# Soft-capped attention and a leaky MLP on one core: grouped score steps, another layout for batch 1's q and k, and weight bounds from squares

## The chip, the cores and the metric

The kernel runs on one core of a Trainium2 chip. The metric is the device time of one execution in microseconds (us); the time of before is the median of three runs.

## The reference

```python
scores = scale * np.matmul(q, k.transpose(0, 1, 3, 2))   # 4 batches x 12 heads, 448 x 448, head_dim 64
scores = cap * np.tanh(scores / cap)
attn = np.exp(scores - scores.max(-1, keepdims=True))
attn = attn / (attn.sum(-1, keepdims=True) + 1e-09)
x = np.matmul(attn, v)            # then (4, 448, 768) -> 1792 tokens of 768
h = x @ w_in                      # 768 x 2048
g = np.maximum(h, 0.0) + alpha * np.minimum(h, 0.0)
out = (g @ w_out).astype(np.float32)
```

All inputs but the weights and alpha are float32; w_in and w_out arrive as float64 and are turned into float32 in the kernel with shifts on VectorE (`to_f32`, lines 973 to 997).

## The kernel before, in words

**Precision.** The large products (`mm1` with w_in, line 878, and `mm2` with w_out, line 920) multiply numbers that are split into a high and a low 16-bit part, three products for each. Weights, x and the hidden values are first scaled by powers of two. So each operand needs a bound of its size: of q and k for batches 2 and 3, of v for each batch (`vbatch`, line 485), and of each 128-wide chunk of the weights (`norms`, line 999).

**Bounds of the weights.** For a chunk of 128 x 768, six bf16 products of the chunk with itself on TensorE (`gram`, line 1003) leave a 128 x 128 matrix in PSUM; ScalarE then sums its absolute values row by row (`bound`, line 387, with an accumulator). There are 32 chunks, 16 of w_in and 16 of w_out, in eight groups of four. The bound of v is the largest absolute value of each load, by a VectorE reduction (line 499), six for each batch.

**From 128 partitions to one number.** `allmax` (line 395) turns a column of maxima with a transpose on TensorE (line 408), reduces on VectorE (line 404), and sends the result to all partitions with a float32 product with `ones` (line 411). It is called 22 times.

**Attention.** Two heads make a unit (a "pair", six for each batch). A score step computes 128 rows of both heads of a unit (`step`, line 560): products on TensorE into one of two PSUM buffers, tanh on ScalarE (line 579), a maximum on VectorE (line 583), exp on ScalarE (line 590). The 64 rows left over in a unit of 448 rows are put together with those of the next unit in one step with four quadrants ("tail"). There are 42 steps in batches 0 and 1, in float32 (`scores_32`, line 547), and 42 in batches 2 and 3, in split form (`scores_3`, line 553). Each step is one operation of the plan on TensorE. For batches 0 and 1 q and k are loaded as (head, position, d) and turned by float32 products of 64 columns with the identity (`turn`, line 510), two heads at a time in the two column halves of the array: eight such products for 448 rows of q or k. The attention weights are turned either on TensorE (`turn_32`, line 658, batch 0 and the first two units of batch 1) or, from there on, split on ScalarE, VectorE and GpSimd and turned by DMA (`turn_split`, line 635).

**Splitting.** A split in "direct" form is a scaled high part (any of three engines) and one VectorE operation for the low part (line 437). In the other form it is a scaling in place, a copy, and a subtraction that VectorE or GpSimd may take (lines 646 to 648 and 691 to 693). The shares `PA`, `QA` and `VA` (lines 68, 69 and 77) say what part of the blocks of the attention weights, of q and k, and of v takes the direct form.

**The order.** The program is written out ahead by a list scheduler (`Plan`, line 92). Each operation has a priority (`prio` plus an offset `OFF[tag]`, line 82), estimated durations for each engine that may do it, and regions that it reads and writes. At each moment every engine takes the ready operation of the lowest number. SP issues all loads and stores in the order that the plan gives. Where TensorE has nothing to do in the first part, the plan puts in products that nobody reads (`fill`, line 1146).

**Stages.** Batch 0's attention (with w_in, w_out and batch 1's attention beside it), then `mm1` of batch 0, and so on, with the next batch's attention beside the products of the last.

Of the kernel before, what the change touches and what calls it, by code (L numbers as in the profile page):

```python
# [10 lines left out]
F32 = mybir.dt.float32  # L11
# [14 lines left out]
VM = 0  # L26
NM = 1.0
MQ = 3
AQ = 3
PEN = 9557.32  # L30
PEN2 = -1671.74
PENP = 5200.84
B0_P = 93.34
LD_P = -164.74
LO_P = 1000.92
MM_P = 4281.34
X_P = 315.24
ST_P = 16.4
ST1_P = -45.43
PV_P = 472.96  # L40
QK_P = -151.82
V_P = 260.72
WI_P = 61.01
WI_S = -61.06
A_S = 2.7
MM1_P = 318.9
WO_P = -214.34
WO_S = 99.12
WT_P = -410.5
WT_S = 70.95  # L50
B1_P = 663.99
B_S = 274.91
EVAC_P = -855.04
# [28 lines left out]
OFF = [-65.0, 6.9, 224.8, 851.3, 36.2, -180.9, 44.9, -286.1, -175.0, -265.3, 4.4, 117.7, -15.8, 9.2, -390.3, 0.0, 45.0, -62.9, -109.4, 120.6, -265.2, -349.8, 24.6, -515.1, -49.0, 243.8, -1013.8, -3.5, 43.4, 0.0, -77.0, 123.3, 26.1, 120.4, 29.4, -6.2, 15.4, -212.7, -27.4, 0.0, 60.8, 7.6, 0.0, 254.3, 178.4, 5.0, -87.7, 524.0, 70.1, 161.5, 27.5, -55.8, -195.2, -115.0, 0.0, 126.1, 302.1, -51.9, -333.5, -18.9, 0.5, 53.5, -114.5, -86.3, -14.4, -100.4, 284.8, 177.1, -107.8, 3.9, -157.6, -54.5, 125.4, -8.7, 0.0, 14.8, 0.0, -119.3, 23.0, -192.0, -212.7, -149.3, -12.4, 18.2, 71.8, 186.2, 0.0, -86.2, 0.0, -5.0, 77.7, 438.7, 44.3, 0.0, 0.6, -1145.9, 37.7, -11.3, -250.4, -182.1, -181.5, 256.2, -26.1, -60.8, -11.1, 107.6, -898.5, 92.5, -382.7, -110.3, -4.1, 24.0, 40.1, -4.5, -27.2, 39.1, -77.6, -13.4, 4.7, 0.0, 67.6, 91.6, 107.9, -4.9, 19.1, -11.5, -4.6, 0.0, 19.9, 16.4, 211.6, -17.2, -23.8, 8.2, -0.7, 74.9, 21.2, -96.8, 0.0, -124.2, -8.4, 3.6, -807.4, 16.1, 0.0, -25.4, 0.0, 108.1, -97.6, -0.3, -72.3, 1276.7, 808.9, -325.6, 158.2, -634.9]  # L82
# [9 lines left out]
class Plan:  # L92
# [16 lines left out]
    def op(self, prio, times, fn, r=(), w=(), rows=1.0, port=True, mode=0):  # L109
        o = lambda: None  # L110
        o.prio, o.times, o.fn, o.rows, o.idx, o.port, o.mode = prio + OFF[self.tag], times, fn, rows, len(self.ops), port, mode
# [24 lines left out]
    def order(self):  # L136
# [55 lines left out]
        while todo:  # L192
# [10 lines left out]
            for e in free:  # L203
# [3 lines left out]
                while ready[e]:  # L207
# [4 lines left out]
                    if not fits(o) or e == "dve" and o.port and port["pool"] > now:  # L212
                        skipped.append(item)
                        continue
                    for h in o.handles:
                        if h.slot is None:
                            h.slot = banks.pop(0)
                            used[h.kind] += 1
                            if h.kind == "m":
                                self.line.pop(0)  # L220
# [7 lines left out]
                    elif e == "pe":  # L228
                        free[e] = run_pe(t + (SWITCH if o.mode and o.mode != mode else 0.0), o.rows)
# [37 lines left out]
def kernel(  # L267
# [79 lines left out]
    ones = ct([NF, P], F32, "ones")  # L347
# [9 lines left out]
    junk = ct([P, 512], mybir.dt.uint8, "junk")  # L357
# [29 lines left out]
    def bound(e, o, i, func=AF.Abs):  # L387
        if e == "act":
            nc.scalar.activation(out=junk[:i.shape[0], :i.shape[1]], in_=i, func=func, accum_out=o)
        else:  # L390
            absmax(o, i)

    mxt_no = [0]

    def allmax(prio, src, rows, r, first, w):
# [7 lines left out]
        def reduce(e):  # L403
# [7 lines left out]
        op(prio, {"pe": 310}, lambda e: nc.tensor.matmul(  # L411
            ps_p[h.slot][:, 256:256 + m], ones[:m], diag if m > 1 else top, start=True, stop=True), r=[tr], w=[h])
# [40 lines left out]
    def load(prio, dst, src, b, pair, w):  # L453
        op(prio, {"sp": (550, 1400, 1000)}, lambda e: nc.sync.dma_start(out=dst.rearrange("p (h c) -> p h c", h=2),  # L454
# [8 lines left out]
    def loads32():  # L463
        for pair in range(NPAIR):
            n = 2 * NCH * D
            for i, src in ((4, k), (6, q)):
                o = pair % 3 * n
                t = wpair[i + pair // 3].rearrange("p a b -> p (a b)")[:CP, o:o + n]
                raw32[i, pair] = t, (("wp", i + pair // 3), o, o + n)
                load(QK_P + A_S * pair, t, src, 0, pair, [raw32[i, pair][1]])  # L470
# [13 lines left out]

    def vbatch(b):
# [8 lines left out]
        op(prio, {"dve": 30}, lambda e: nc.vector.memset(t[:, :NPAIR], 0.0), w=[(u.tok, 0, 9)])  # L494
        for pair in range(NPAIR):
            rv, m = vslot(b, pair)
            v0[b, pair] = rv, m
            load(prio + 0.4 * pair, rv, v, b, pair, [m])
            op(prio + 0.4 * pair, {"act": 830} if b < VM else {"dve": 680}, lambda e, pair=pair, rv=rv: bound(e, t[:CP, pair:pair + 1], rv, AF.Square),
               r=[m], w=[(u.tok, pair, pair + 1)] + [("junk", 0, 1)] * (b < VM), port=False)  # L500
# [37 lines left out]
    def t0_slot(i):  # L538

        if i % 5 < 4:  # L540
# [3 lines left out]
                    [(("g", r // 2), r % 2 * GW + lo, r % 2 * GW + lo + 2 * CP) for r in range(a, a + 8)])  # L544
        return pt32[:, -2 * S:].rearrange("p (c j k) -> p c j k", c=2, j=NCH), [("pt", 10 * S, 12 * S)]
# [13 lines left out]

    def step(u, pr, col, routes, scale):  # L560
# [4 lines left out]
        units = [r[0] for r in routes[0]]  # L565

        def products(e):
            for fns in zip(*(u.scores(s, x, *r) for x in range(2) for r in routes[x])):
                for fn in fns:
                    fn()  # L570

# [625 lines left out]
```

## Time and profile before

| | |
|---|---|
| median of 3 runs | 683.25 us (683.14 to 683.63) |
| the profiled execution, its own time | 686.12 us |
| its span | 684.3 us |
| granted clock, mean | 0.995 |
| instructions | 13548 |

How to read the rows further down: "busy" is the time in which at least one instruction of the engine was under way; for TensorE ("PE") matmuls overlap, so the cost of a group of matmuls is better read from the time between its start and the start of the next group in the timeline. A float32 product appears as two records. DVE is VectorE, ACT is ScalarE, POOL is GpSimd, SPq is the queue of SyncE, which issues the DMAs.

### The profile page before, as it was taken

The numbers are of one execution on the slowest core, as the hardware profiler recorded it, in microseconds if no ns is written. First come the engines' busy times: TensorE is split into PE (matmuls) and PEld (weight loads), VectorE is DVE, ScalarE is ACT, GpSimd is POOL, SyncE is SP. The second block draws the span as 40 slices with busy tenths as digits, with TensorE's granted clock in tenths as the row PEclk, the third lists the DMA queues.
The fourth block names the chain that finished last, engine by engine and source line by source line (L and its number), as shares of the span: only waits on it lengthen the run. The fifth ranks groups of instructions, "written<-read, shape, count | busy, mean of one in ns | idle before, by whom it ended". The sixth has DMA issues, their size and how long they took to land.

```text
span 684.3 us, 13548 instructions
## 1 busy us (share of the span) xinstructions
PE 666.8 (97%) x5151; PEld 413.4 (60%) x5151; DVE 481.7 (70%) x922; ACT 395.4 (58%) x853; POOL 237.4 (35%) x354
## 2 busy tenths in 40 slices
PE   8998998989999999999999999999999999999997
PEld 7787776768877555544555555545455555555664
DVE  3998999999989977687898577878877504441000
ACT  5887797885857666476575546756756513331100
POOL 1145755335656532264433234444432200000000
PEclk9999999999999999999999999999999999999999
DMA  8995674366664369937749989766466640000011
GB/s 176 292 323 154 203 235 115 102 194 178 159 125 85 39 140 205 185 62 137 139 77 179 197 167 181 139 139 122 91 136 116 106 73 22 1 0 1 24 46 24
DMA packets 181792, 87.07 MB, mean 127 GB/s; under 512 B 145312, under 2 KB 178016, under 8 KB 181728
## 3 DMA queue, kind: packets, MB, share of 16 engines
q1 hardware_dynamic: 181728, 86.22, 56.9%
q8 instruction: 40, 0.66, 0.4%
q14 instruction: 24, 0.20, 0.1%
HBM read 45.82 MB, written 5.51 MB: 75 GB/s over the span
## 4 chain that ended last, share of the span: by engine, by line
PE 66%; DVE 19%; DMA 6%; ACT 3%; SPq 3%; issue 2%; POOL 1%; ACTq 0%; DVEq 0%; POOLq 0%
PE p L886 27%; PE p L927 24%; PE p L711 4%; DVE mxs L583 4%; PE s L557 3%; DMA ptall<-pw 3%; PE p L738 2%; DVE wp L437 2%; PE s L551 2%; SPq L454 1%; DVE wi L437 1%; DVE wp L992 1%; DVE wp L986 1%; PE p L515 1%; SPq L847 1%
## 5 line engine op out<-in xcount | busy, mean ns | idle before, releaser
L886 PE MATMUL p<-xring,wi 128*128 128x448 f16 (+2 forms) x1440 | 225.8, 315 | 0.3 <-DVE gr L896 0.3
L927 PE MATMUL p<-wp,gall 128*128 128x384 f16 x1344 | 224.9, 326 | 0.4 <-DVE gr L896 0.4
L886 PEld LDWEIGHTS <-wi 128*128 128x128 f16 x1440 | 134.7, 98 | 84.2 <-issue 5.7
L927 PEld LDWEIGHTS <-gall 128*128 128x128 f16 x1344 | 129.2, 98 | 90.7 <-issue 7.3
L590 ACT ACTIVATE tall<-tall,mxs 128x448 f32<-128x448 f32 x126 | 82.7, 659 | 15.1 <-POOL mxs L585 9.8
L896 DVE SCALAR_TENSOR_TENSOR gr<-p,ca_g,gr 128x448 f32<-128x448 f32 (+2 forms) x80 | 46.9, 586 | 47.7 <-ACT gr L427 47.4
L585 POOL TENSOR_SCALAR mxs<-mxs,small 128x2 f32<-128x2 f32 x62 | 33.3, 537 | 99.1 <-DVE mxs L583 69.3
L583 DVE TENSOR_REDUCE mxs<-tall 128x2 f32<-128x896 f32 x63 | 66.9, 1075 | 1.0 <-ACT tall L579 0.9
L427 ACT ACTIVATE gr<-p,cs_g 128x448 f32<-128x448 f32 (+2 forms) x63 | 34.7, 551 | 56.0 <-PE p L886 53.3
L434 POOL TENSOR_TENSOR gall<-gr,gall 128x192 f16<-128x192 f32 (+4 forms) x52 | 45.0, 869 | 33.0 <-ACT gall L421 21.7
L437 DVE SCALAR_TENSOR_TENSOR pw<-tall,rr,pw 128x448 f16<-128x448 f32 x56 | 41.1, 735 | 14.1 <-ACT pw L427 12.4
L579 ACT ACTIVATE tall<-s,ams 128x896 f32<-128x896 f32 x42 | 41.1, 1000 | 14.6 <-PE s L557 6.0
L434 POOL TENSOR_TENSOR pw<-tall,pw 128x448 f16<-128x448 f32 x33 | 38.7, 1173 | 26.6 <-ACT pw L421 25.1
L427 ACT ACTIVATE wp<-p,small 128x384 f32<-128x384 f32 x19 | 10.9, 576 | 55.3 <-PE p L927 55.3
L421 ACT ACTIVATE gall<-gr 128x384 f16<-128x384 f32 (+4 forms) x51 | 24.2, 477 | 30.7 <-DVE gr L896 30.6
L711 PE MATMUL p<-ptall,vs 112*64 112x448 f16 x384 | 40.3, 355 | 0.2 <-issue 0.2
L607 POOL TENSOR_SCALAR rr<-sums 128x2 f32<-128x2 f32 (+2 forms) x70 | 27.6, 394 | 29.5 <-ACT tall L590 22.3
L427 ACT ACTIVATE pw<-tall,rr 128x448 f16<-128x448 f32 x27 | 17.9, 665 | 27.2 <-DMA ptall<-pw 23.2
L711 PEld LDWEIGHTS <-vs 112*64 112x64 f16 x384 | 21.2, 110 | 17.3 <-issue 3.7
L434 DVE TENSOR_TENSOR gall<-gr,gall 128x384 f16<-128x384 f32 (+4 forms) x60 | 28.4, 478 | 4.1 <-ACT gall L421 1.6
L421 ACT ACTIVATE ptall<-p 112x512 f32<-112x512 f32 (+1 forms) x48 | 26.3, 580 | 6.5 <-PE p L665 5.3
L421 ACT ACTIVATE pw<-tall 128x448 f16<-128x448 f32 x37 | 21.2, 574 | 14.5 <-DMA ptall<-pw 12.6
(155 smaller groups left out, 961.5 us busy)
## 6 DMA issues: line engine op xcount, KB each, us to landing
wp<-in_moe_w_in_dram SPq DMA_DIRECT2D x16, 768.0 KB, 7.6
wp<-in_moe_w_out_dram SPq DMA_DIRECT2D x16, 768.0 KB, 5.2
rvs<-in_v_dram SPq DMA_DIRECT2D x38, 224.0 KB, 3.4
rqk<-in_q_dram SPq DMA_DIRECT2D x18, 224.0 KB, 3.2
rqk<-in_k_dram SPq DMA_DIRECT2D x18, 224.0 KB, 3.4
ptall<-pw SPq DMA_TRANSPOSE x128, 3.2
wp<-in_k_dram SPq DMA_DIRECT2D x6, 224.0 KB, 5.7
wp<-in_q_dram SPq DMA_DIRECT2D x6, 224.0 KB, 6.0
```

The lines of the kernel that those rows point to most:

```text
L421: nc.scalar.activation(out=o, in_=i, func=AF.Copy)
L427: nc.scalar.activation(out=o, in_=i, func=AF.Copy, scale=s)
L434: (nc.gpsimd if e == "pool" else nc.vector).tensor_tensor(out=o, in0=a, in1=b, op=ALU.subtract)
L437: nc.vector.scalar_tensor_tensor(out=o, in0=i, scalar=s, in1=hi, op0=ALU.mult, op1=ALU.subtract)
L579: op(pr, {"act": (152 if reg else 245) + 377 * 2}, lambda e: nc.scalar.activation(out=t, in_=s[:, :, :S].rearrange("p c (j k) -> p c j k", ...
L583: op(pr, {"dve": 136 + 469 * 2}, lambda e: nc.vector.tensor_reduce(out=mt, in_=t, axis=AX.XY, op=ALU.max), r=tr, w=[mr], port=False)
L585: op(pr, {"dve": 200, "pool": 265}, lambda e: (nc.gpsimd if e == "pool" else nc.vector).tensor_scalar(out=mt, in0=mt, scalar1=ncap, scalar ...
L590: nc.scalar.activation(out=t[:, x], in_=t[:, x], func=AF.Exp, scale=capr, bias=mt[:, x:x + 1], accum_out=sums[:, u.idx % 3, col + x:col + ...
L711: nc.tensor.matmul(pv[x * D:(x + 1) * D, :n], vs[:, z, c:c + D], u.pt[x][:CP, y * NCH + kc], start=(i == 0), stop=(i == len(prods) - 1))
L886: nc.tensor.matmul(ps_p[h.slot][:, :n], w[:, z, kk, :], x[:, d, o:o + n], start=(kk == 0 and z == d), stop=(kk == NPAIR - 1 and z == 1))
L896: op(pr, {"dve": 198 + 1.07 * n}, lambda e: nc.vector.scalar_tensor_tensor(out=t, in0=ps_p[h.slot][:, :n], scalar=ca_g[:, j:j + 1], in1=t, ...
L927: nc.tensor.matmul(ps_p[h.slot][:, :NH], g[j][:, d, t * P:(t + 1) * P], w[:, z, hf * NH:(hf + 1) * NH], start=(j == 0 and z == d), stop=(j ...
```

## The change

- One operation of the plan computes the products of up to two score steps in a row (`products`, with `PAIR = (1, 1)`); tails stay single and come after the group that holds the second unit's first step. The turns of the attention weights are put into the plan unit by unit.
- The plan, when TensorE would change the shape of its tiles, takes a ready operation of the present shape whose priority is at most `SAME` behind.
- Batch 1's q and k are loaded with the two heads side by side, with one DMA per head, and turned by four transposes.
- The weight bounds: 24 of 32 chunks (half of w_in, all of w_out) are squared and summed on ScalarE; the other eight keep their products, and a VectorE maximum reads them.
- The bound of v for batches 0 and 1 (`VM = 2`) comes from products of v with itself on TensorE and one VectorE maximum for several loads.
- `ones` and the second operand of its product are bf16.
- `QA` 1 to 0, `VA` 1 to 0.5, `PA` 0.5 to 0.25: fewer splits in direct form.
- Each load of q, k, v and of the weights has a priority offset of its own; all constants and offsets of the plan have new values.
- The stores of the fourth token tile are one DMA instead of two; `cap` is loaded from ScalarE's queue.

```diff
-VM = 0
+VM = 2
-QA = 1.0
-VA = 1.0
+QA = 0
+VA = 0.5
+SAME = 209.56
+LOAD_C = (600, 1400, 950)
+SPLIT_W = (0.5, 1)
+PAIR = (1, 1)
-PA = 0.5
+PA = 0.25
...
+                    if e == "pe" and mode and o.mode != mode:
+                        top = item[0] + SAME
+                        while ready[e] and ready[e][0][0] <= top:
+                            x = heapq.heappop(ready[e])
+                            if x[2].mode == mode and fits(x[2]):
+                                skipped.append(item)
+                                item, o = x, x[2]
+                                break
+                            skipped.append(x)
...
-    ones = ct([NF, P], F32, "ones")
+    ones = ct([NF, P], BF16, "ones")
...
-        op(prio, {"pe": 310}, lambda e: nc.tensor.matmul(
-            ps_p[h.slot][:, 256:256 + m], ones[:m], diag if m > 1 else top, start=True, stop=True), r=[tr], w=[h])
+        op(prio, {"pe": 100}, lambda e: nc.tensor.matmul(
+            ps_p[h.slot][:, 256:256 + m], ones[:m], (diag if m > 1 else top).bitcast(BF16).rearrange("p (m t) -> p m t", t=2)[:, :, 1],
+            start=True, stop=True), r=[tr], w=[h])
...
+    def gram_v(prio, o, w, tops):
+
+        h = plan.handle("n")
+
+        def gram(e):
+            for i, (top, _) in enumerate(tops):
+                for c in range(NCH):
+                    nc.tensor.matmul(ps_p[h.slot][:, :P], top[:, c, :, 1], top[:, c, :, 1],
+                                     start=(i == c == 0), stop=(i == len(tops) - 1 and c == NCH - 1))
+
+        op(prio, {"pe": 230 * len(tops)}, gram, r=[m for _, m in tops], w=[h], rows=0.875)
+        op(prio, {"dve": 280}, lambda e: absmax(o, ps_p[h.slot][:, :P]), r=[h], w=[w], port=False)
...
+            if b < VM:
+                tops.append((rv.bitcast(BF16).rearrange("p (c f t) -> p c f t", f=P, t=2), m))
+                if len(tops) == (2 if b else NPAIR):
+                    gram_v(prio + 0.4 * pair, t[:, pair:pair + 1], (u.tok, pair, pair + 1), tops)
+                    tops = []
+                continue
...
+    def products(pr, steps):
+
+        sr = [(("S", (step_no[0] + z) % 2), 0, 1) for z in range(len(steps))]
+
+        def run(e, i0=step_no[0]):
+            for z, (u, _, _, routes, _) in enumerate(steps):
+                s = ps_s[(i0 + z) % 2]
+                for fns in zip(*(u.scores(s, x, *r) for x in range(2) for r in routes[x])):
+                    for fn in fns:
+                        fn()
...
+        groups = []
+        while line:
+            k_ = 2 if PAIR[us[0].b > 0] else 1
+            groups.append(line[:k_])
+            line = line[k_:]
+        if m:
+            a, tail = us[0], slice(n - m, n)
+            at = next(i for i, g_ in enumerate(groups) if g_[-1][0] is us[1] or (i + 1 < len(groups) and groups[i + 1][0][0] is us[1]))
+            groups.insert(at + 1, [(a, a.prio + st_p * nf, nf, [[(v, y, slice(x * QP, (x + 1) * QP), tail) for x, v in enumerate(us)] for y in range(2)], a.joint)])
...
+        for dst, src, w in ((rq, q, rqr), (rk, k, rkr)):
+            if scores32:
+                for h in range(2):
+                    op(prio - 20, {"sp": LOAD_C}, lambda e, h=h, dst=dst, src=src: nc.sync.dma_start(
+                        out=dst.rearrange("p (c h d) -> p h c d", h=2, d=D)[:, h],
+                        in_=src[b, 2 * pair + h].rearrange("(p c) d -> p c d", c=NCH)), w=[(w[0], w[1] + h / 2, w[1] + (h + 1) / 2)])
+            else:
+                load(prio - 20, dst, src, b, pair, [w])
...
-                op(prio - i, {"pe": 205 * NCH}, lambda e, h=h, raw=raw: turn(h, raw, 0, NCH), r=[rr_, identr], w=[h, w], rows=0.7, mode=1)
+                def turn_c(e, h=h, raw=raw):
+                    for c in range(NCH):
+                        nc.tensor.transpose(ps_p[h.slot][:, c * CP:(c + 1) * CP], raw[:, c * P:(c + 1) * P], ident[:CP, :CP])
+
+                op(prio - i, {"pe": TURN * NCH}, turn_c, r=[rr_, identr], w=[h, w])
...
+        grams = []
+        for i, (flat, fr) in enumerate(flats):
+            sq = share(norm_no[0] % NF, SPLIT_W[norm_no[0] // NF])
+            norm_no[0] += 1
+            if sq:
+                op(prio, {"act": 195 + 0.833 * DM}, lambda e, i=i, flat=flat: nc.scalar.activation(
+                    out=junk, in_=flat, func=AF.Square, accum_out=n[:, i:i + 1]), r=[fr], w=[(nr[0], nr[1] + i, nr[1] + i + 1), ("junk", 0, 1)], port=False)
+            else:
+                grams.append((i, flat, fr))
+        if not grams:
+            return
...
+        op(prio, {"dve": 150 + 130 * m}, lambda e: absmax(n[:, i0:i0 + st * (m - 1) + 1:st], ps_p[h.slot][:, :m * P].rearrange("p (m f) -> p m f", f=P)),
+           r=[h], w=[(nr[0], nr[1] + i, nr[1] + i + 1) for i, _, _ in grams], port=False)
...
+        if t == 3:
+            p0, both_b = 3 * P - (NCH - 1) * CP, out[(b - 1) * S:(b + 1) * S].rearrange("(i p c) e -> c i p e", i=2, c=NCH)
+            op(EVAC_P, {"sp": (550, 1000, 800)}, lambda e: nc.sync.dma_start(
+                out=both_b[NCH - 1, :, p0:, a], in_=osb[:, a]), r=[osr])
+            return
...
-    nc.sync.dma_start(out=capt, in_=cap.to_broadcast([P, 1]))
+    nc.scalar.dma_start(out=capt, in_=cap.to_broadcast([P, 1]))
```

## Rows read from the trace of the kernel before

**Rows 1.** Chain that ended last, by engine, from the page.
```profile
PE 66%; DVE 19%; DMA 6%; ACT 3%; SPq 3%; issue 2%; POOL 1%; ACTq 0%; DVEq 0%; POOLq 0%
```
**Rows 2.** Busy time by stretches: stretch and length, engines, clock, DMA.
```profile
20.00:240.00 220.00, 210.83 (x2153) 162.62 (x2145) 205.19 (x357) 167.40 (x405) 115.12 (x140) 0.98 0.62 169
240.00:560.00 320.00, 318.04 (x2081) 168.66 (x2081) 240.85 (x479) 191.30 (x381) 120.10 (x200) 1.00 0.72 138
```
**Rows 3.** Timeline of PE: start, length, line, operands; batch 1's turns and neighbours.
```profile
97.90 0.38 PE L411 MATMUL p<-mxt,ones 4*128 4x4 f32 x2
98.21 0.65 PE L665 MATMUL p<-ident,gall 128*112 128x128 f32 x4
98.79 1.03 PE L551 MATMUL s<-qkTs 64*128 64x224 f32 x8
...
124.84 0.99 PE L515 MATMUL p<-ident,rqk 112*64 112x112 f32 x16
125.76 0.52 PE L1006 MATMUL p<-wp 128*128 128x128 bf16 x6
126.12 1.65 PE L886 MATMUL p<-xring,wi 128*128 128x192 f16 x18
```
**Rows 4.** Timeline of PE: batches 0 and 1, first and last of 37 score runs.
```profile
8.00 1.03 PE L551 MATMUL s<-tall,qkTs 64*128 64x224 f32 x8
...
94.11 1.78 PE L551 MATMUL s<-qkTs 64*128 64x224 f32 x16
95.82 0.27 PE L408 MATMUL p<-ident,n_wi 128*4 128x128 f32 x1
...
241.52 1.03 PE L551 MATMUL s<-qkTs 64*128 64x224 f32 x8 [1.22 <-ACT tall L579]
242.48 9.92 PE L927 MATMUL p<-wp,gall 128*128 128x384 f16 x60
```
**Rows 5.** Timeline of PE: batches 2 and 3, first and last of 24 score runs; allmax.
```profile
260.94 1.31 PE L557 MATMUL s<-qkTs 64*128 64x448 f16 x12
...
267.13 0.27 PE L408 MATMUL p<-ident,vam 128*1 128x128 f32 x1
267.24 2.11 PE L927 MATMUL p<-wp,gall 128*128 128x384 f16 x12
...
523.94 1.44 PE L557 MATMUL s<-qkTs 64*64 64x448 f16 x18
...
527.36 1.31 PE L557 MATMUL s<-qkTs 64*128 64x448 f16 x12
```
**Rows 6.** Groups of DVE by line: count, busy, mean ns, idle before.
```profile
L385 DVE TENSOR_REDUCE vam<-rvs 112x1 f32<-112x512 f32 x20 | 13.4, 675 | 4.6 <-DMA rvs<-in_v_dram 4.4
L437 DVE SCALAR_TENSOR_TENSOR pw<-tall,rr,pw 128x448 f16<-128x448 f32 x10 | 7.4, 748 | 0.0
L748 DVE TENSOR_TENSOR xs<-p,xs 128x256 f32<-128x256 f32 x6 | 2.4, 410 | 0.0
```
**Rows 7.** Groups of ACT by line.
```profile
L389 ACT ACTIVATE junk<-p 128x128 uint8<-128x128 f32 x32 | 8.7, 271 | 0.7 <-PE p L1006 0.5
L389 ACT ACTIVATION_READ_ACCUMULATOR junk<-p 128x1 f32 x32 | 6.4, 200 | 0.0
L427 ACT ACTIVATE wp<-wp,s_wo 128x768 f16<-128x768 f32 x13 | 12.1, 934 | 6.1 <-DVE wp L437 6.1
L421 ACT ACT_TABLE_LOAD x1 | 1.3, 1283 | 0.7 <-PEq L1181 0.7
```
**Rows 8.** POOL's subtraction, and SP's waits and issue of q and k.
```profile
L434 POOL TENSOR_TENSOR pw<-tall,pw 128x448 f16<-128x448 f32 x33 | 38.7, 1173 | 26.6 <-ACT pw L421 25.1 <-DVE pw L423 0.7
SPq L454 <- PE p L515: 21.4, 10, 6.3
rqk<-in_k_dram SPq DMA_DIRECT2D x18, 224.0 KB, 3.4
```
**Rows 9.** Timeline of SP's queue at the start.
```profile
0.72 0.60 SPq L1152 DMA_DIRECT2D small<-in_cap_dram  x1
```

More of the change, by code (lines that the diff above doesn't have):

```diff
@@ L25 @@
 GUARD = 1e-9 * math.exp(EXP_BIAS)
-VM = 0
-NM = 1.0
+VM = 2
 MQ = 3
 AQ = 3
[L30 to L53, printed above, removed]
+PEN = 11684.16
+PEN2 = -1614.45
+PENP = 10077.68
+B0_P = 174.12
+LD_P = -270.26
+LO_P = 908.9
+MM_P = 2448.92
+X_P = 475.19
+ST_P = 63.05
+ST1_P = -43.26
+PV_P = 390.15
+QK_P = -78.75
+V_P = 196.4
+WI_P = 21.53
+WI_S = -63.55
+A_S = 5.03
+MM1_P = 480.9
+WO_P = -182.63
+WO_S = 86.83
+WT_P = -1018.45
+WT_S = 131.8
+B1_P = 701.09
+B_S = 239.81
+EVAC_P = -930.96
 LAT = 35.0
@@ L228, in order @@
                     elif e == "pe":
-                        free[e] = run_pe(t + (SWITCH if o.mode and o.mode != mode else 0.0), o.rows)
+                        free[e] = run_pe(t + (SWITCH + o.first if o.mode != mode else 0.0), o.rows)
                         mode = o.mode
@@ L558, in scores_3 @@
                                                     start=(z == 0 and w == 2), stop=(w == 3))
+    def products(pr, steps):
[6 more added lines that the diff above has]
+                        fn()
+        exact = steps[0][0].scores is scores_32
+        t = sum((SCORE if exact else SCORE_3)[len(routes[0]) - 1] for _, _, _, routes, _ in steps)
+        op(pr, {"pe": t}, run, r=[x for _, _, _, routes, _ in steps for r in routes[0] for x in r[0].qk], w=sr,
+           mode=1 + len(steps[0][3][0]), first=104.0 if exact and len(steps[0][3][0]) == 1 else 50.0 if exact else 10.0)
     def step(u, pr, col, routes, scale):
@@ L598, in step @@
             factors(u, pr, col, col + 2)
-        later = []
+        now, wait = [], []
         for x in range(2):
-            later += (turn_split if u.dma else turn_32)(u, pr, routes[x], t[:, x], tr, col + x)
-        return later
+            more = []
+            wait.append(lambda more=more: [fn() for fn in more])
+            now.append(lambda x=x, more=more: more.extend((turn_split if u.dma else turn_32)(u, pr, routes[x], t[:, x], trs[x], col + x)))
+        return now, wait
     def factors(u, pr, a, z):
@@ L614, in units @@
         nf, m = 2 * (n // P), n % P
+        line = []
         for i, u in enumerate(us):
-            plan.tag = 3 * u.idx + 1
             for c in range(0, nf, 2):
                 cols = slice(c // 2 * P, c // 2 * P + P)
-                step(u, u.prio + st_p * c, c, [[(u, y, slice(0, P), cols)] for y in range(2)], u.scale)
-            later, z = [], nf
-            if m and i == 0:
-                tail = slice(n - m, n)
-                z += 2
-                later = step(u, u.prio + st_p * nf, nf, [[(v, y, slice(x * QP, (x + 1) * QP), tail) for x, v in enumerate(us)] for y in range(2)], u.joint)
@@ L625, in units @@
-            if not u.dma:
-                factors(u, u.prio + st_p * nf, 0, z)
-            plan.tag = 3 * u.idx + 2
-            finish(u)
-            plan.tag = 3 * u.idx + 1
-            for fn in later:
-                fn()
+                line.append((u, u.prio + st_p * c, c, [[(u, y, slice(0, P), cols)] for y in range(2)], u.scale))
+        groups = []
[3 more added lines that the diff above has]
+            line = line[k_:]
```

123 lines of the change are left out of this document (70 added, 53 removed).

## The prediction

> **What bounds the kernel now.** The chain of waits, by engine, comes first [rows 1]: TensorE carries 66% of it, VectorE 19%, DMA 6%. Then the busy time by stretches [rows 2] shows where each applies. From 240 to 560 us TensorE is busy 318.0 of 320, at full granted clock, with VectorE at 240.9 and ScalarE at 191.3: there the end is TensorE's work and nothing else. From 20 to 240 us, call it the first part, TensorE has 210.8 of 220 and VectorE 205.2, so two engines compete for the bound; TensorE is the fuller one. The mean granted clock of the first part is 0.98: of the two levels, 1.2 and 2.4 GHz, the lower one had a small part, 0.02 x 220 = 4.4 us of full-speed work lost. The rest (560 us to the end) is products that the change leaves alone. So a term counts fully where TensorE is alone, and between a part and the whole in the first part. The reader prices TensorE from the timeline, start of a group to start of the next, since matmuls overlap.
>
> **The parts on TensorE.**
> *Turns of batch 1.* Twelve turns of eight float32 products: 124.84 to 125.76, 0.92 us each [rows 3]. Four transposes instead: the nearest row, four transposes of the attention weights, goes from 98.21 to 98.79, 0.58, with a change of tile shape behind it [rows 3]; bounds 0.4 (112 columns instead of 128, no change) and 0.6. I take 0.5: 12 x 0.42 = 5.0 us off, all in the first part.
> *Weight bounds.* A chunk's six products take 125.76 to 126.12, 0.36 [rows 3]; 24 of 32 go: 8.6 off, first part.
> *Bounds of v.* Twelve loads of batches 0 and 1, four products each, at 0.36/6: 12 x 0.24 = 2.9 added, first part.
> *allmax.* Its float32 product takes 97.90 to 98.21, 0.31 [rows 3]. No row shows the bf16 one; a transpose of as small a result takes 267.13 to 267.24, 0.11 [rows 5], and below nothing is excluded, since a matmul stays. Between 0.05 and 0.31 I take 0.11: 22 x 0.2 = 4.4 off, 9 of them in the first part (1.8), 13 behind it (2.6).
> *Score steps two at a time.* A step alone takes 241.52 to 242.48, 0.96; two in a row 94.11 to 95.82, 1.71 [rows 4], so joining two saves 0.2. In batches 0 and 1 the timeline has 37 separate runs for 42 steps, from 8.00 to 241.52 [rows 4]; the new groups are 24: 13 x 0.2 = 2.6 off. In batches 2 and 3 it has 24 runs for 42 steps already, such as two steps (260.94) and a tail with a step (523.94) [rows 5], and the new code makes four groups for each of six pairs of units, 24 again: nothing. The rule for the present tile shape can save a change here and there, 0.1 to 0.2 each; I take nothing.
> Sum on TensorE: -5.0 - 8.6 + 2.9 - 4.4 - 2.6 = -17.7, of it -15.1 in the first part and -2.6 behind.
>
> **The parts elsewhere.** VectorE loses twelve reductions of v (0.675 each [rows 6]: 8.1) and gains eight maxima from PSUM, four for v and four for weights; the nearest row, 256 columns read from PSUM, is 0.41 [rows 6], so 3.3 at most: net -4.8. Fewer direct splits take work from VectorE to GpSimd; of the ten direct blocks in the first part (7.4 us [rows 6]) half go, 3.7 if GpSimd takes the subtractions (1.17 each against 0.75 [rows 6, 8]), nothing if VectorE keeps them. So VectorE sheds 4.8 to 8.5 of 205.2. Behind the first part the same shift is costed at nothing: GpSimd has 120.1 of 320 [rows 2] and TensorE always has a group of the large products ready; with that cover gone, a later low part would show as idle TensorE before L711 or L557.
> ScalarE drops 32 sums from PSUM (0.271 + 0.200 [rows 7]: 15.1) and takes 24 squares over 768 columns; the nearest row of that width is 0.934 [rows 7], plus 0.2 for the accumulator: 27.2. Net +12.1 on 167.4 of 220: it still has room, but squares stand in one queue with the copies that free PSUM.
> *Table set.* The trace shows one table load, 1.283 us, for tanh, exp, copy and abs together [rows 7]; no square is in it. The Trainium skill (ScalarE: Activation LUTs, Table sets) says that a set holds cheap functions as filler, and its list there names relu, copy, identity and abs but not square; a switch costs about 2.66 us with the drain by its account. By that rule, were square missing, the sum would not be a gain at all; I keep it as a rival.
> *Loads.* Twelve more DMAs on SP, each some 0.5 us of issue, in a queue that has time: it waits 21.4 us for TensorE to free the buffers of q and k [rows 8], so the turns set those loads and not the reverse. The pieces written shrink to 64 floats, 256 bytes. A load lands in 3.4 us now [rows 8]; between as now and twice as long I take as now, hidden, since the next load waits for its buffer anyway.
> The Trainium skill (DMA: Bandwidth & Descriptors, Specifications) wants at least 512 bytes for line rate, which speaks against this layout; with twice 3.4 us on six pairs and nothing hidden, the sum would be 20 us worse and the change a loss. No row here shows such a load.
> *Start and end.* `cap` leaves SP's queue ahead of the first q and k: 0.6 of issue [rows 9], bounds 0 and 0.6, I take 0.6. Of the last two stores one goes; an issue is at most 0.6 by the same row: between 0 and 0.6 I take 0.5, the issue being last in the chain.
> The new priorities and offsets reorder everything. That can't be priced from rows: between nothing and the whole loss of the first part (9.2 idle, some 4 of clock); I take nothing.
>
> **The sum.** Were VectorE alone the bound of the first part, it would shrink by 4.8 / 0.93 = 5.2 us; were TensorE, by 15.1. Since TensorE is the fuller one (210.8 against 205.2), I go two thirds of the way: 11.8. With 2.6 + 0.6 + 0.5 that is 15.5. The profiled execution took 686.12 (span 684.3), 2.9 above the median of the runs; the same is taken off both: 670.6 for such an execution, and 683.25 - 15.5 = **667.75**, say 667.8, for the median. Its own range: 662 to 674.
>
> **The rivals.**
> *TensorE all the way (15%).* The first part sheds all 15.1, and the new order takes part of the 13 us lost there too. For it: TensorE is the fuller engine [rows 2]. Against it: less work on one of two balanced engines usually opens gaps. 683.25 - 18.8 = 664.5 without, and with half the loss 658; 657 to 662.
> *The first part is held by VectorE and ScalarE (23%).* TensorE's savings turn into idle or fill products. For it: VectorE's 19% of the chain [rows 1] and ScalarE's +12. The first part shrinks by 5.2 at most, or grows by up to 3: 674 to 682.5, middle 677. The upper end is also where the pairing and the bf16 product do nothing, so that the change does not do what it says. Of the 23, 18 are faster by more than 0.2%, 3 within, 2 slower.
> *Squares hold up PSUM (4%), the slower side.* Place: ScalarE's queue in the first part, 24 x 1.13 = 27.2 us of squares, each ahead of a copy from PSUM that TensorE waits for. If all is passed on, 667.8 + 27 = 695; it decides from 15.5/27.2, 57%, passed on. Against it: ScalarE is 3% of the chain now [rows 1], and the 15.1 us of sums stood in the same queue.
> *A table load before and behind each square (4%).* 24 x 2 x 1.283 = 61.6 us of ScalarE, which would then need 167.4 + 12.1 + 61.6 = 241 us in a part that lasts 220: with the present 96% of the busiest engine 251, 31 longer, less the 3.7 elsewhere: about 710. That is the place where the page on tables would be seen; the trace so far, four functions in one load, speaks against it.
>
> **How the numbers follow.** Forecast 54%, TensorE all the way 15, held first part 23, the two of ScalarE 8. About 0.2%, 1.4 us, is what a measurement of this kernel can tell from no change. Faster: 54 + 15 + 18 = 87%. Same: 3. Slower: 2 + 8 = 10. The range leaves out the two of ScalarE (8), the upper end of the held part beyond 680 (7) and a little below 657 (3): 657 to 680, which also holds the bounds of the terms.
>
> **What would show it.** Right: L515 on rqk gone and 48 more transposes with some 0.5 us per turn; 48 records of L1006's kind left for eight chunks; allmax's product at 0.1 us; fewer, longer runs of the scores in the first 240 us and as many as now behind; from the start of batch 2's scores on, a saving of 2 to 3 us only; squares near 1.1 us and one table load. Wrong: idle of TensorE or fill products in the first part well above 9.2 us of idle would mean that VectorE or ScalarE holds it; an end of the first part more than 17 us earlier would mean that the order, which I gave nothing, was worth more than the work; a shorter stretch behind it by over 5 us would mean that I miscounted the changes of tile shape.

## The result, and the profile after

Before: 683.43 us, after: 689.12 us (medians of 20 runs each); ratio 1.009, 95% interval 1.007 to 1.011. The change costs 5.7 us where 15.5 were forecast as a gain: the wrong sign, and outside the range of 657 to 680.

| | |
|---|---|
| the profiled execution of after, its own time | 690.83 us |
| its span | 689.1 us |
| granted clock, mean | 0.988 |
| instructions | 13358 |

First the rows that answer to those of before. The chain of waits by engine, from the page of after, answers to [rows 1], and the busy time by stretches (columns as there) to [rows 2]:

```profile
PE 68%; DVE 14%; DMA 10%; ACT 4%; issue 2%; SPq 1%; POOL 0%; ACTq 0%; DVEq 0%; POOLq 0%
```

```profile
20.00:240.00 220.00, 210.58 (x2110) 164.27 (x2108) 207.31 (x375) 191.66 (x421) 118.88 (x161) 1.00 0.65 170
240.00:560.00 320.00, 309.11 (x2031) 164.87 (x2030) 224.32 (x433) 197.61 (x398) 142.83 (x222) 0.98 0.74 134
```

DMA went from 6% to 10% of the chain. The first part looks healthy: a granted clock of 1.00, TensorE as full as before. The stretch behind it, which before was TensorE's work and nothing else, now has 11 us without TensorE and a clock of 0.98. So the loss is where the forecast had only small terms.

The parts themselves came out near their prices. The timeline of after's TensorE answers to [rows 3 to 5]; the last row is of the start:

```profile
95.95 0.60 PE L904 MATMUL p<-ident,rqk 112*128 112x112 f32 x4
96.48 1.78 PE L582 MATMUL s<-tall,qkTs 64*128 64x224 f32 x16
98.19 1.08 PE L734 MATMUL p<-ident,ptall 128*112 128x128 f32 x8
...
261.98 0.17 PE L418 MATMUL p<-mxt,ones 2*128 2x2 bf16 x1
262.09 4.07 PE L1006 MATMUL p<-wp,gall 128*128 128x384 f16 x24
```

```profile
14.57 1.78 PE L582 MATMUL s<-tall,qkTs 64*128 64x224 f32 x15
```

A turn takes 95.95 to 96.48, 0.53 (0.5 taken); two score steps 1.71, as before; allmax's product 0.11 (0.11 taken). The first score, however, starts at 14.57 instead of 8.00. Groups of instructions of after, and two lines of its DMA issues, answer to [rows 6 to 8]:

```profile
L398 DVE TENSOR_REDUCE n_wi<-p 128x2 f32<-128x256 f32 x4 | 1.7, 417 | 0.0
L1089 ACT ACTIVATE junk<-wp 128x768 uint8<-128x768 f32 x17 | 14.4, 845 | 3.9 <-DVE wp L1075 2.1 <-issue 1.2 <-DVE rr L652 0.5
L1089 ACT ACTIVATION_READ_ACCUMULATOR junk<-wp 128x1 f32 x17 | 3.4, 198 | 0.0
L429 ACT ACT_TABLE_LOAD x1 | 1.3, 1283 | 1.3 <-PEq L1272 1.3
```

```profile
rqk<-in_q_dram SPq DMA_DIRECT2D x12, 112.0 KB, 4.5
rqk<-in_k_dram SPq DMA_DIRECT2D x12, 112.0 KB, 4.3
```

A maximum from PSUM 0.417 (0.41 taken), a square 0.845 and 0.198 (0.934 and 0.2 taken), one table load. A load of half the bytes in 256-byte pieces lands in 4.3 to 4.5 instead of about 3.4 (in the first of the kernels below in 4.9 and 5.9), hidden as forecast: TensorE waits for none of them.

**Where TensorE stood still.** The timeline of after from 430 us, with SyncE's queue, GpSimd and TensorE:

```profile
430.82 10.38 PE L965 MATMUL p<-xring,wi 128*128 128x448 f16 x54
432.11 0.67 SPq L1028 DMA_DIRECT2D out_dram<-wp  x1
432.87 7.09 SPq L720 DMA_TRANSPOSE ptall<-pw  x1
...
445.78 0.56 POOL L431 CAST pw<-tall 128x448 f16<-128x448 f32 x1 [10.44 <-DMA ptall<-pw]
...
450.24 0.34 PE L415 MATMUL p<-ident,small 112*2 112x112 f32 x1 [9.04 <-DVE small L398]
450.38 5.63 PE L965 MATMUL p<-xring,wi 128*128 128x448 f16 x18
```

The chain of waits of after has, in that place:

```profile
432.87 12.77 DMA ptall<-pw
```

and the busy time by short stretches of after (three in the gap by themselves, and at last three of the end), then of before:

```profile
430.00:440.00 10.00, 10.00 (x56) 5.28 (x54) 5.88 (x9) 7.40 (x16) 3.62 (x6) 1.00 1.22 90
440.00:450.00 10.00, 1.20 (x7) 0.39 (x5) 3.63 (x6) 2.37 (x4) 2.99 (x5) 0.72 0.90 184
450.00:460.00 10.00, 9.76 (x64) 4.50 (x68) 6.86 (x16) 4.15 (x7) 3.76 (x6) 0.77 0.36 66
...
438.00:440.00 2.00, 2.00 (x12) 1.07 (x11) 0.00 (x0) 0.12 (x1) 0.00 (x0) 1.00 0.13 35
440.00:442.00 2.00, 1.20 (x7) 0.39 (x5) 0.00 (x0) 0.00 (x0) 0.00 (x0) 1.00 0.13 52
446.00:448.00 2.00, 0.00 (x0) 0.00 (x0) 1.63 (x4) 0.83 (x2) 1.89 (x3) 0.50 1.30 123
...
676.00:680.00 4.00, 2.93 (x19) 1.56 (x16) 0.00 (x0) 1.16 (x2) 0.00 (x0) 1.00 0.04 9
680.00:684.00 4.00, 0.00 (x0) 0.00 (x0) 0.00 (x0) 0.00 (x0) 0.00 (x0) 0.90 0.13 42
684.00:688.00 4.00, 0.00 (x0) 0.00 (x0) 0.00 (x0) 0.00 (x0) 0.00 (x0) 0.50 0.13 47
```

```profile
440.00:450.00 10.00, 10.00 (x65) 5.05 (x64) 8.87 (x17) 4.21 (x9) 4.66 (x7) 1.00 0.64 119
...
680.00:684.00 4.00, 0.00 (x0) 0.00 (x0) 0.00 (x0) 0.58 (x1) 0.00 (x0) 1.00 0.41 88
```

Read them in this order. At 432.11 SyncE issues L1028, the store of the fourth token tile, which the change writes for both batches in one DMA. The DMA transpose issued right behind it, at 432.87, lands 12.77 us later (3.2 is the median of its 128 on the page). GpSimd waits 10.4 us for it, VectorE and ScalarE behind that, and at last TensorE 9.0 us; its next 18 products then take 5.63, partly at the lower level of the clock (0.50 from 446 to 448, 0.77 on the mean from 450 to 460), where the 54 ahead of the gap took 10.38 at the full one, 3.46 for each 18. At the end the last products finish at 678.93 and the span at 689.1: 10.2 us of tail, against 4.4 before (679.90 to 684.3). In that tail the DMA column stands at 0.13 from 680 to 688. The column is a mean over sixteen engines, and 2/16 is 0.125: two engines move the whole store, at 42 to 47 GB/s. The gap in the middle has the same mark: from 438 to 442 the column is 0.13 again, at 35 to 52 GB/s: two engines at work and fourteen idle, and the transpose lands behind that.

Why two can be read off the access pattern: "c i p e" with c fixed leaves the batch, of size 2, as the slowest dimension. The Trainium skill (DMA: Bandwidth & Descriptors, Why a DMA increments its semaphore by 16 and not by 1) says that a DMA takes the largest number of engines, up to sixteen, that divides the slowest dimension larger than one on both sides: two here, 16 for a store of 64 rows. The 0.13 agrees with the two; the 16 no row shows by itself.

### The profile page after: what moved, and what is told of

It is laid out like the page before. It is cut to its first block, busy times and chain, and to the rows that moved or that the text cites. A ratio compares the mean times of both kernels' runs of the same rounds, so it can differ in the third digit from the quotient of the medians.

```text
span 689.1 us, 13358 instructions
## 1 busy us (share of the span) xinstructions
PE 656.9 (95%) x5042; PEld 412.0 (60%) x5042; DVE 464.7 (67%) x884; ACT 419.2 (61%) x867; POOL 264.2 (38%) x394
## 4 chain that ended last, share of the span: by engine, by line
PE 68%; DVE 14%; DMA 10%; ACT 4%; issue 2%; SPq 1%; POOL 0%; ACTq 0%; DVEq 0%; POOLq 0%
PE p L1006 24%; PE p L965 24%; DMA ptall<-pw 8%; PE p L780 5%; PE s L588 3%; DVE mxs L623 3%; PE s L582 2%; PE p L807 2%; DVE wp L1069 2%; PE p L734 2%; DVE wp L1075 2%; PE p L1240 2%; PE p L546 2%; DVE wp L1065 1%; DMA wp<-in_moe_w_out_dram 1%
## 5 line engine op out<-in xcount | busy, mean ns | idle before, releaser
L442 POOL TENSOR_TENSOR pw<-tall,pw 128x448 f16<-128x448 f32 x42 | 47.1, 1123 | 26.0 <-ACT pw L429 21.1
L435 ACT ACTIVATE wp<-p,small 128x384 f32<-128x384 f32 x21 | 12.1, 577 | 67.2 <-PE p L1006 67.2
L435 ACT ACTIVATE gr<-p,cs_g 128x448 f32<-128x448 f32 (+2 forms) x55 | 30.3, 550 | 33.9 <-PE p L965 33.6
L649 POOL TENSOR_SCALAR rr<-sums 128x2 f32<-128x2 f32 (+2 forms) x70 | 23.5, 336 | 61.2 <-ACT tall L630 44.0
L429 ACT ACTIVATE pw<-tall 128x448 f16<-128x448 f32 x53 | 30.1, 572 | 24.0 <-DMA ptall<-pw 22.5
L429 ACT ACTIVATE gall<-gr 128x384 f16<-128x384 f32 (+4 forms) x61 | 28.0, 465 | 22.7 <-DVE gr L975 22.4
L442 DVE TENSOR_TENSOR pw<-tall,pw 128x448 f16<-128x448 f32 x42 | 29.1, 692 | 18.8 <-POOL pw L431 10.0
L442 POOL TENSOR_TENSOR gall<-gr,gall 128x256 f16<-128x256 f32 (+4 forms) x47 | 35.3, 754 | 9.4 <-ACT gall L429 7.7
L435 ACT ACTIVATE tall<-tall,rr 128x448 f32<-128x448 f32 x41 | 26.7, 663 | 19.0 <-DVE rr L652 19.0
L442 DVE TENSOR_TENSOR gall<-gr,gall 128x384 f16<-128x384 f32 (+4 forms) x65 | 31.6, 488 | 8.8 <-ACT gall L429 5.1
L588 PE MATMUL s<-qkTs 64*128 64x448 f16 (+1 forms) x288 | 28.1, 352 | 0.0
```

Of the source, the lines that this page charges most:

```text
L429: nc.scalar.activation(out=o, in_=i, func=AF.Copy)
L435: nc.scalar.activation(out=o, in_=i, func=AF.Copy, scale=s)
L442: (nc.gpsimd if e == "pool" else nc.vector).tensor_tensor(out=o, in0=a, in1=b, op=ALU.subtract)
L588: yield lambda z=z, w=w: nc.tensor.matmul(s[rows, x, :S], q[a, z * S + cols.start:z * S + cols.stop], q[a, w * S:(w + 1) * S], start=(z == ...
```

## The experiments

The theory: the merged store alone makes the change slower, in the middle through the transposes and at the end through its own length. The rivals: the loss lies in the new order, in the start, in the squares or in the work of TensorE.

**The merged store in two, the rest and the order as after.**

```diff
-            op(EVAC_P, {"sp": (550, 1000, 800)}, lambda e: nc.sync.dma_start(
-                out=both_b[NCH - 1, :, p0:, a], in_=osb[:, a]), r=[osr])
+            op(EVAC_P, {"sp": (550, 1000, 800)}, lambda e: [nc.sync.dma_start(
+                out=both_b[NCH - 1, i, p0:, a], in_=osb[i * QP:(i + 1) * QP, a]) for i in range(2)], r=[osr])
```

> The changed kernel in the same order on every engine, but each merged store of the fourth token tile (batch index outermost, 2 x 64 rows) written as two DMAs of 64 rows, as before. Theory (the merged store moves on two of the 16 DMA engines, and the transpose behind it in SP's queue is held): the gap of all engines near 441 to 450 us (9.0 us of TensorE) and the long end (10.2 us from TensorE's last product to the end of the span, 4.3 before) go: about 689.1 - 9 - 6 = 674 us. Rival (the middle gap is a pile-up of transposes that the new order makes, the store only lengthens the end): 683 us, gap still there.

Measured: 672.81, ratio 0.983 (0.981 to 0.985), 16.3 us under after (some 17 by the two ratios, 1.009 and 0.983, as each was measured beside runs of before of its own). The timeline of SyncE's queue and the windows of this kernel, the last one from its end:

```profile
430.03 1.18 SPq L1028 DMA_DIRECT2D out_dram<-wp  x2
431.31 1.33 SPq L720 DMA_TRANSPOSE ptall<-pw  x1
```

```profile
440.00:450.00 10.00, 10.00 (x80) 4.88 (x78) 8.68 (x18) 7.34 (x14) 4.66 (x9) 1.00 0.63 116
...
668.00:668.50 0.50, 0.00 (x0) 0.00 (x0) 0.00 (x0) 0.00 (x0) 0.00 (x0) 1.00 0.61 132
```

The gap is gone, the tail is 4.5 us (666.36 to 670.9), and a store of 192 KB lands in 2.9 us. The last stores now reach a DMA share of 0.61, about ten engines on the mean of that half microsecond, where the merged one stood at 0.13. The theory holds, and this version beats both kernels.

**The kernel before with the merged store alone, plan kept.**

```diff
+        if t == 3:
+            p0, both_b = 3 * P - (NCH - 1) * CP, out[(b - 1) * S:(b + 1) * S].rearrange("(i p c) e -> c i p e", i=2, c=NCH)
+            op(EVAC_P, {"sp": (510, 1000, 800)}, lambda e: nc.sync.dma_start(
+                out=both_b[NCH - 1, :, p0:, a], in_=osb[:, a]), r=[osr])
+            op(EVAC_P, {"sp": (510, 1000, 800)}, lambda e: None, r=[osr])
+            return
...
         for rows in [out_rows(b, t * P, P)] if t < 3 else [out_rows(b - 1, 3 * P, QP), out_rows(b, 3 * P, QP)]:
```

> The kernel before with the merged store alone, the two operations of the plan kept so that its order stays. Theory: the end grows from 4.3 to about 10 us and a gap shows behind the store of batches 0 and 1 where it meets transposes: 689 to 698 us. Rival (the store is harmless by itself): 683.4 us.

Measured: 693.59 beside 684.18, ratio 1.014 (1.011 to 1.017). Its windows:

```profile
440.00:450.00 10.00, 7.36 (x50) 3.65 (x48) 4.44 (x9) 3.04 (x8) 1.30 (x2) 1.00 0.27 65
...
684.00:688.00 4.00, 0.00 (x0) 0.00 (x0) 0.00 (x0) 0.00 (x0) 0.00 (x0) 0.69 0.13 50
```

The same two marks in the old program: a tail 6 us longer and a gap of some 3 us, together about the 9.4 measured. In the new order the gap is 9 us and costs the clock as well.

**The merged store on ScalarE's queue, the rest as after.**

```diff
-            op(EVAC_P, {"sp": (550, 1000, 800)}, lambda e: nc.sync.dma_start(
+            op(EVAC_P, {"sp": (550, 1000, 800)}, lambda e: nc.scalar.dma_start(
                 out=both_b[NCH - 1, :, p0:, a], in_=osb[:, a]), r=[osr])
```

> The changed kernel with its merged stores as they are (two rows of the outermost dimension in one DMA), but issued on ScalarE's queue instead of SyncE's; the order is kept otherwise. 689.1 us with the store on SyncE, 672.8 with two stores. If the gap of all engines near 441 to 450 us comes from the DMA transposes queued behind the merged store on the same queue, it goes, and only the slow store at the end stays: 689.1 - 9 = 680, within 2. If it comes from the two DMA engines that the store keeps busy, whichever queue it is on, the gap stays: 688 to 690. In either case the span ends with some 6 us more of tail than with two stores.

Measured: 688.48, ratio 1.008 (1.005 to 1.010). The timeline of this kernel:

```profile
430.57 1.12 ACTq L1028 DMA_DIRECT2D out_dram<-wp  x1
...
442.82 0.56 POOL L431 CAST pw<-tall 128x448 f16<-128x448 f32 x1 [8.26 <-DMA ptall<-pw]
...
447.27 0.34 PE L415 MATMUL p<-ident,small 112*2 112x112 f32 x1 [7.56 <-DVE small L398]
```

The gap stays with the store on another queue than the transposes. So the order of issue on SyncE isn't the cause. What the three runs leave is the two engines: with the store on them the transposes wait whichever queue it was issued from, with the store spread they don't.

**Batch 0's q and k first, and single score steps, both planned anew**, on the kernel with two stores. The edits: a priority lower by 20000 for the twelve loads, and `PAIR`.

```diff
-                load(QK_P + A_S * pair, t, src, 0, pair, [raw32[i, pair][1]])
+                load(QK_P - 20000 + A_S * pair, t, src, 0, pair, [raw32[i, pair][1]])
```

> As e1, with batch 0's twelve loads of q and k ahead of all others (their priorities lowered by 20000; everything else is planned anew). Theory that the new load order costs the start (11 us of fill products in the first 20 us, 4.2 before): 4 to 7 us less than e1. Rival (VectorE and ScalarE hold the first part, so what TensorE gets early is idle later): within 2 us of e1.

```diff
-PAIR = (1, 1)
+PAIR = (0, 0)
```

> As e1, with PAIR = (0, 0): each score step its own operation. If the pairing is worth what the prediction said (13 joins of 0.2 us, all on TensorE's bound): 2 to 3 us more than e1. Rival (already joined by the order, or hidden): within 1 us of e1.

Measured: 701.84 (ratio 1.027, 1.024 to 1.031) and 692.61 (1.012, 1.009 to 1.014), 29 and 20 us over their base: both missed. Neither is the price of its part. From the first product with w_out to the end of the span all take 458 to 464 us, and that product comes at 207.34 with two stores, at 227.12 with single steps, at 240.27 with the loads first: the planner made a worse first part. Its offsets were found for another list of operations; that this is why was not shown. So the next kernels keep the order of every instruction and change only its body.

**`ones` in float32, order kept**, on the kernel with two stores.

```diff
-    ones = ct([NF, P], BF16, "ones")
+    ones = ct([NF, P], F32, "ones")
...
-            ps_p[h.slot][:, 256:256 + m], ones[:m], (diag if m > 1 else top).bitcast(BF16).rearrange("p (m t) -> p m t", t=2)[:, :, 1],
+            ps_p[h.slot][:, 256:256 + m], ones[:m], diag if m > 1 else top,
```

> The changed kernel with the merged store split in two (672.8 us, ratio 0.983 to the kernel before), instruction order kept on every engine, with `ones` and the operand of its product back in float32: 22 products at some 0.31 instead of 0.11 us. If TensorE's work decides all the way, the time rises by 22 x 0.2 = 4.4, to 677; if the first part has slack that takes up its 9, only the 13 behind it count, 2.6, to 675.5; if TensorE waits for VectorE's reduction around each of these products anyway, nothing: 672.8 within 0.7.

Measured: 675.73, ratio 0.989 (0.985 to 0.993), 2.9 us over the base, with some 2.5 to either side; the first product with w_out comes at 207.61, 0.3 later, and the span ends 2.2 later (673.1). By the traces the product costs about what was forecast and counts behind the first part; the medians alone allow all 4.4 as well.

**The turns as eight products, order kept**, on the same base.

```diff
-                        nc.tensor.transpose(ps_p[h.slot][:, c * CP:(c + 1) * CP], raw[:, c * P:(c + 1) * P], ident[:CP, :CP])
+                        _ = [nc.tensor.matmul(ps_p[h.slot][x * D:(x + 1) * D, c * CP:(c + 1) * CP], raw[:, c * P + x * D:c * P + (x + 1) * D], ident[:CP, :CP], start=True, stop=True) for x in range(2)]
```

> The same base (672.8 us), instruction order kept, with each of the twelve turns of batch 1's q and k made by eight float32 products of 64 columns instead of four transposes; the loads stay as they are. The turns take 0.53 now and took 0.92: 12 x 0.39 = 4.7 more work for TensorE, all in the first part. If TensorE holds the first part: 677.5. If VectorE holds it, the work goes into TensorE's gaps: 672.8 within 0.7. Between the two, the share passed on says how much of the first part TensorE holds; my prediction took two thirds, 676.

Measured: 678.56, ratio 0.992 (0.989 to 0.995). Two windows each, split at the first product with w_out, of the base and of this kernel:

```profile
0.00:207.34 207.34, 195.76 (x2112) 159.75 (x2113) 186.29 (x338) 172.63 (x382) 102.04 (x148) 1.00 0.71 187
207.34:670.90 463.56, 456.61 (x2932) 249.81 (x2929) 276.62 (x547) 248.78 (x487) 163.91 (x247) 1.00 0.55 104
```

```profile
0.00:210.21 210.21, 202.10 (x2256) 165.55 (x2257) 185.14 (x338) 172.53 (x381) 102.07 (x148) 0.99 0.71 184
210.21:674.30 464.09, 456.55 (x2932) 249.47 (x2929) 278.23 (x547) 249.12 (x487) 163.60 (x247) 1.00 0.55 104
```

In the two traces the first part grows by 2.9 for 4.7 us of added work, 61%, close to the two thirds taken. By the medians it is 5.7, all of the work and more; the interval on that is about 2.5 us to either side, and the execution traced was the fastest of the eight, so the share lies between 0.6 and 1, by the medians nearer to 1.

**Squares over 8 of 768 columns, order kept**, on the same base.

```diff
-                    out=junk, in_=flat, func=AF.Square, accum_out=n[:, i:i + 1]), r=[fr], w=[(nr[0], nr[1] + i, nr[1] + i + 1), ("junk", 0, 1)], port=False)
+                    out=junk[:, :8], in_=flat[:, :8], func=AF.Square, accum_out=n[:, i:i + 1]), r=[fr], w=[(nr[0], nr[1] + i, nr[1] + i + 1), ("junk", 0, 1)], port=False)
```

> The same base (672.8 us), instruction order kept; the 24 squares of ScalarE read 8 of 768 columns, so this kernel leaves out most of the sums behind the weight bounds. That takes some 24 x 0.7 = 17 us of work from ScalarE in the first 200 us. If ScalarE's queue holds the first part (the squares stand ahead of copies from PSUM that TensorE waits for), the time falls by 4 us or more, to under 669. If ScalarE has room, as costed in the prediction: 672.8 within 1.

Measured: 673.54, ratio 0.984 (0.980 to 0.988), no gain (one of up to some 2 us can't be told; 4 or more was expected if ScalarE held the first part). Its window, against ScalarE's 192.22 in the same stretch of the base:

```profile
20.00:240.00 220.00, 210.80 (x2086) 164.10 (x2085) 207.19 (x376) 179.21 (x420) 120.93 (x162) 1.00 0.67 173
```

Thirteen us taken from ScalarE move the first product with w_out by 0.3 (207.03 against 207.34): the squares hold nothing up that this can tell.

**The start, order kept**, on the same base: q and k ahead of w_in and v in SyncE's queue; that, with the 190 fill products behind the first 32 taken out; and the fills taken out alone (`front` marks the twelve loads, the fourth entry is empty for a fill, the first is its planned start in ns).

```diff
-        for _, fn, e in self.order():
+        for _, fn, e, o in sorted(self.order(), key=lambda x: not (x[3] and x[3].front)):
...
+        for _, fn, e, o in sorted((x for x in self.order() if x[3] or x[0] < 5000), key=lambda x: not (x[3] and x[3].front)):
...
+        for _, fn, e, o in (x for x in self.order() if x[3] or x[0] < 5000):
```

> The changed kernel with the merged store in two (672.8 us), the instruction order of every engine kept; only on SyncE the twelve loads of batch 0's q and k go ahead of w_in and v. The fill products stay in TensorE's queue (16.3 us of them, 32 records at the start and 190 behind), so the first part can lose no more than TensorE's idle of the first 20 us, 1.5, while v and w_in come up to 8 issues of 0.5 later. If the loads' order matters only through the fills that it made the plan put in: 672.8 within 2. If the loads themselves hold the start: 671 or less.

> As the one before, with the 190 fill products behind the first 32 taken out (records of nobody's result, 190 x 0.07 = 13 us of TensorE). If the start of the changed kernel is late because q and k come behind w_in and v, the chain moves up by most of the 7 us of fills that it has more than the kernel before in the first 20 us: 665 to 668. If v, w_in or the other engines hold the start, TensorE idles where the fills were: 672.8 within 1.5. Rival on the slower side: without fills the granted clock falls in the first 60 us (it is 1.00 there now); with it at the lower level over some 10 us, up to 5 us are lost: 675 to 678.

> The same base (672.8 us) with the 190 fill products behind the first 32 taken out, and the loads where they are. If the fills only stand where TensorE waits anyway: 672.8 within 1, with the same first w_out product near 207 us. If they hold up real work behind them in TensorE's queue: up to 3 us less. If they keep the granted clock up: it falls in the first 60 us and the time rises by 2 to 5.

Measured: 682.05 (ratio 0.999, 0.997 to 1.000), 678.41 (0.994, 0.991 to 0.996) and 670.76 (0.983, 0.980 to 0.986). The first missed by 9, the second came 5.6 above the base where a gain of 5 to 8 was expected. TensorE's waits, first 60 us, of the first and of the second:

```profile
PE p L1100 <- DVE wi L1075: 6.4, 1, 6.4
```

```profile
PE p L1100 <- DVE wi L1075: 10.4, 1, 10.4
```

A weight-bound product stands early in TensorE's queue and its chunk of w_in now leaves at 8.98 instead of 2.17. The loads and TensorE's queue were made for each other: in the base TensorE's longest wait of that stretch is 1.4. The second kernel's granted clock did fall (0.87 in the first 20 us), as its third case had it, but the first, with its fills, is the slower of the two. The fills alone cost nothing that can be told from the base (0.983 both): they stood where TensorE waits anyway.

**The kernel before with bf16 `ones` alone, order kept.**

```diff
-    ones = ct([NF, P], F32, "ones")
+    ones = ct([NF, P], BF16, "ones")
...
-            ps_p[h.slot][:, 256:256 + m], ones[:m], diag if m > 1 else top, start=True, stop=True), r=[tr], w=[h])
+            ps_p[h.slot][:, 256:256 + m], ones[:m], (diag if m > 1 else top).bitcast(BF16).rearrange("p (m t) -> p m t", t=2)[:, :, 1], start=True, stop=True), r=[tr], w=[h])
```

> The kernel before with its plan and order kept, and `ones` with the operand of its 22 products in bf16: this part of the change alone. 0.31 to 0.11 us each: 13 of them behind the first part give 2.6, the other 9 give 1.8 more if TensorE's work holds the first part and nothing if the gaps there swallow it. So 679.8 to 681.6 against 684.2 of the kernel before. If the products hide beside VectorE's reductions everywhere: 684 within 0.7.

Measured: 680.94 beside 683.05 on that chip, ratio 0.997 (0.996 to 0.999): 1.8 us, with an interval from 0.7 to 2.9. That holds the 2.6 of the thirteen products behind the first part, and not the 4.4 of all 22.

## Why the prediction was wrong, step by step

**The step that failed** is in the term on start and end: "Of the last two stores one goes; an issue is at most 0.6 by the same row: between 0 and 0.6 I take 0.5, the issue being last in the chain." It priced the issue and not the transfer, and took both sides' bounds from an issue alone. In its place stands a loss of 16.3 us in the new program (689.12 against 672.81) and of 9.4 in the old one. It also looked at the last store only, while the same line runs for batches 0 and 1 in the middle of the program, with DMA transposes behind it. The prediction names the same page of the Trainium skill, DMA: Bandwidth & Descriptors (Specifications), for its rule on piece size, which turned out hidden, and not for this one. No rival had this mechanism: the one on the slower side by ScalarE is refuted by the narrow squares, the one by table loads by the single load of 1.283 us, and the two on the gaining side left the store as it was.

**Without that step** the time is 672.8, inside the range and inside the forecast's own 662 to 674; of the 15.0 us that the other terms make, 11.4 came (684.18 less 672.81). That the sum comes so near is in part luck, as the terms below show. The stretches are of the two traces, whose spans differ by 13.4, as the profiled execution of before was above its median.

*The first part* was to shrink by 11.8 and shrank by 14.8: the first product with w_out moved from 222.17 to 207.34. The reason was not the one given, for part of that work only moved behind. TensorE's groups behind that product, first of the kernel before, then with two stores:

```profile
L927 PE MATMUL p<-wp,gall 128*128 128x384 f16 x1344 | 224.9, 326 | 0.4 <-DVE gr L896 0.4
...
L711 PE MATMUL p<-ptall,vs 112*64 112x448 f16 x336 | 35.3, 355 | 0.2 <-issue 0.2
...
L411 PE MATMUL p<-mxt,ones 2*128 2x2 f32 (+1 forms) x26 | 4.9, 256 | 0.0
...
L551 PE MATMUL s<-qkTs 64*128 64x224 f32 x8 | 1.0, 375 | 1.2 <-ACT tall L579 1.2
```

```profile
L1006 PE MATMUL p<-wp,gall 128*128 128x384 f16 x1344 | 223.4, 326 | 0.0
...
L780 PE MATMUL p<-ptall,vs 112*64 112x448 f16 x360 | 38.3, 355 | 1.4 <-DMA ptall<-pw 1.4
...
L582 PE MATMUL s<-qkTs 64*128 64x224 f32 (+1 forms) x48 | 4.6, 362 | 0.0
...
L418 PE MATMUL p<-mxt,ones 2*128 2x2 bf16 (+1 forms) x13 | 2.2, 173 | 0.0
```

Five score steps of batch 1 (8 to 48 records, 3.6 us) and the products with v of one unit (336 to 360, 3.0 us) now come behind it. So 14.8 less 6.6, 8.2 us, is what the first part gave in the traces, between the two bounds of 5.2 and 15.1 and below the 11.8. Part of it is the execution that was traced: its clock of 0.98 [rows 2] was not the rule, for the kernel before with bf16 `ones`, in the same order, has 1.00 there. With the 2.0 us that the medians differ less than the spans (11.4 against 13.4), some 6 us are left, an estimate. The two thirds are neither refuted nor shown: the turns passed on 61% in the traces and nearer to all by the medians.

Where the rest went, the rows show in part. The planner put in 222 fill products (16.3 us) in place of 69 (6.7 us), 148 of them in the first 20 us, and the first score comes later: some 10 us of what TensorE shed came back as fill. The prediction's sign for that was that VectorE or ScalarE holds the first part. For VectorE speaks the stretch from 60 to 120 us, where it is busy 59.53 of 60 with two stores (54.52 before) and TensorE 56.71 (55.11); against it, that most fills stand in the first 20 us, where VectorE is busy 8.40. So that rival may be right in part; no run parts it from the late start, whose own price isn't shown either: without the fills the time stays, and with the loads moved it grows. "I take nothing" for the new order left all this out, and its size stays open.

*Behind it* 2.6 was to be gained and the stretch grew by 1.4 (462.13 to 463.56). The 2.6 holds: allmax's products went from 4.9 to 2.2, and float32 `ones` bring back 2.9, within 2.5 to either side. The 6.6 of moved work hides it, and some 2.6 of gain behind the first part is left that the rows put to no term.

*Costed at nothing, and so it was:* the loads in pieces of 256 bytes, the squares in ScalarE's queue, GpSimd's larger share (142.83 of 320 against 120.10). ScalarE's own term was too small: over the span it is busy 421.41 with two stores and 395.36 before, 26 more where 12.1 were taken, and the squares explain 10 of that (24 x 1.04 less the 15.1 of sums). The fewer direct splits, costed on VectorE and GpSimd alone, are the likely rest; it was not tried, and by the narrow squares ScalarE had the room.

Not tried: the weight bounds, the bound of v and the shares of direct splits, each undone in a kept order; and why the transposes wait as long as the store runs, beyond that they do so with the store on either queue. A merged store with sixteen or more in its slowest dimension was not tried either.

## What to carry over

Merging two DMAs saves an issue and can cost the spread: read the slowest dimension of both sides before pricing it, and in a trace read a DMA share of 2/16 or so beside idle engines as a transfer on a few engines. Price a store by what is queued behind it in the middle of a program, not only by its tail. And undo a part of a planned kernel in the order that the plan gave: a new plan moved the time by 20 to 29 us, several times any part.

## What the runs showed of the hardware that was not expected

A store of 384 KB on two DMA engines (DMA share 0.13) held up DMA transposes from either of two queues: 12.77 us for one behind a store from SyncE's own queue, where 3.2 is the median, and a wait of 8.3 us with the store on ScalarE's. The gap costs twice, since the granted clock, 1.00 up to 440 us, is 0.72 on the mean of the ten us of the standstill (0.50, the lower of the two levels, from 446 to 448), and the first 18 products behind it take 5.63 instead of 3.46.
